# SwiGLU feed-forward on one core: the first 256 tokens of x loaded plainly and transposed on TensorE instead of by DMA

## The chip, the core and the metric

One core of one Trainium2 chip runs the kernel in a single launch. The metric is device time in microseconds (us). The kernel before takes 121.7 us, the median of three runs (121.63 to 121.72). Engines are named as the profile names them: PE is TensorE's matmuls, PEld its weight loads, DVE is VectorE, ACT is ScalarE, POOL is GpSimd, and SP is SyncE, which here only issues DMAs.

## The reference

```python
B, S, D, F = 1, 2048, 512, 1376        # everything in bfloat16
def reference(x, w_gate, w_up, w_down):
    g = silu(x @ w_gate)
    u = x @ w_up
    return (g * u) @ w_down
```

## The kernel before, in words

**Layout.** TensorE sums over the partition axis, so the kernel keeps x transposed in SBUF: xT_sb holds 4 blocks of 128 features (dk = 0 to 3) by 2048 tokens. The gate and up weights lie beside each other in w_sb, 4 blocks of 128 features each. The hidden activations hT_sb have hidden features on partitions, so they serve as the stationary side of the second product directly.

**Order of the work.** Tokens are taken in 4 chunks of 512. For each chunk and each of 10 hidden tiles of 128 features there is a gate group and an up group: four matmuls each, one per dk, 128 x 512, in one PSUM bank (line 260, in gu_matmuls). ACT takes the silu of the gate bank (line 215), DVE multiplies it with the up bank into hT_sb (line 222). The last 96 hidden features go in extra groups (lines 287 and 298). Then come 16 output tiles of 128 tokens, 11 matmuls each over the hidden features (line 315), a copy to bf16 (line 226, the last in two parts) and a store by SP (line 198). Eight PSUM banks are used in turn. Groups are numbered in the order of PE, and every engine's order is fixed when the program is built; semaphores count finished groups (s_P), finished ACT reads (s_A) and finished DVE results (s_D).

**Loads.** All are issued at the start, from two queues. ACT issues the gate and up weights of hidden tile 0 (wg0, wu0; 128 KB each, line 79). SP issues, in this order: x of tokens 0 to 255 (x0a) and of 256 to 511 (x0b), each as one transposing DMA (line 74); the other weights in slabs of growing size; the other three chunks of x, again as transposing DMAs; and w_down. Each load has a semaphore, and PE waits for it once, in `need`, ahead of the first matmul that reads it.

**The start on TensorE.** While the loads are under way PE multiplies a constant of ones: N_WARM = 9 dummies of 128 x 512 (line 268) and N_WARM_SHORT = 3 of 128 x 128 (line 271), into bank 7, and nothing reads their results. Then the first gate and the first up group run in two halves of 256 tokens:

```python
for n0, n1 in ((0, HT), (HT, SC)):      # HT = 256, SC = 512
    for g in groups[0:2]:               # gate 0, up 0
        gu_matmuls(g, n0, n1)
```

so that gate 0 and up 0 on tokens 0 to 255 need x0a only. From the third group on each matmul has 512 columns and the groups follow each other without a gap.

Of the kernel before, what the change touches and what calls it, by code (L numbers as in the profile page):

```python
# [5 lines left out]
ALU = mybir.AluOpType  # L6
BF16 = mybir.dt.bfloat16
FP32 = mybir.dt.float32

N_WARM = 9  # L10
N_WARM_SHORT = 3


def bass_standalone__swiglu_ffn__prompt_kernel(nc, x, w_gate, w_up, w_down, out):
    _, S, D = x.shape
    F = w_gate.shape[1]
    P = 128
# [4 lines left out]
    SC = 512  # L22
# [2 lines left out]
    NST = S // P  # L25
    LASTA = 384
    HT = SC // 2
    NB = 8
    NSG = 4
    NOS = 3  # L30
# [2 lines left out]
    xf = x[0]  # L33
# [8 lines left out]
    with ExitStack() as es:  # L42
        sb = lambda name, shape, dt: es.enter_context(nc.sbuf_tensor(name, shape, dt))
        ps = lambda name, shape, dt: es.enter_context(nc.psum_tensor(name, shape, dt))
        sem = lambda name: es.enter_context(nc.semaphore(name))

        xT_sb = sb("xT_sb", [P, KD, S], BF16)
# [7 lines left out]
        o_sb = [sb(f"o_sb{i}", [P, D], BF16) for i in range(NOS)]  # L55
        banks = [ps(f"bank{i}", [P, 512], FP32) for i in range(NB)]

        s_P = sem("s_P")
        s_A = sem("s_A")
        s_D = sem("s_D")  # L60
# [3 lines left out]
        def load_sem(name):  # L64
            loads[name] = sem(f"s_{name}")
            return loads[name]

        ones_w = nc.const_aps.tensor(1.0, [P, P], BF16)
        ones_m = nc.const_aps.tensor(1.0, [P, SC], BF16)
# [3 lines left out]
        def load_x(eng, name, t0, t1):  # L73
            eng.dma_start_transpose(
                xT_sb[:, :, t0:t1], xf[t0:t1, :]
            ).then_inc(load_sem(name), 16)
# [15 lines left out]
            load_slab(act, *slabs[0])  # L92

        def loads_on_sync(sp):
            load_x(sp, "x0a", 0, HT)
            load_x(sp, "x0b", HT, SC)
            for a, b in slabs[1:]:
                load_slab(sp, a, b)
            load_w(sp, "wut", w_up, F - (F - 32), F - 32, F)
            for c in range(1, NSC):  # L100
                load_x(sp, f"x{c}", c * SC, (c + 1) * SC)
            sp.dma_start(
                wd_sb[:, 0:NFF, :], w_down[0:NFF * P, :].rearrange("(k p) d -> p k d", p=P)
            ).then_inc(load_sem("wd"), 16)
            sp.dma_start(wd_sb[0:F_LAST, NFF, :], w_down[NFF * P:F, :]).then_inc(load_sem("wdt"), 16)
# [3 lines left out]
        groups = []  # L109
# [3 lines left out]
        def add_group(kind, **what):  # L113
            g = dict(kind=kind, at=len(groups), bank=banks[len(groups) % NB], readers=[], **what)
            groups.append(g)
            return g

        def add_op(eng, g, **what):
            n_read[eng] += 1
            op = dict(g=g, at=n_read[eng], **what)  # L120
            (act_ops if eng == "A" else dve_ops).append(op)
            g["readers"].append((eng, op["at"]))
            return op

        sg_reader = []
        n_sg = 0
# [34 lines left out]
        def plan_y(pi):  # L161
            g = add_group("Y", pi=pi)
            for c in (2 * pi, 2 * pi + 1):
# [4 lines left out]
                )  # L168
                t_ready[c] = d["at"]

        for c in range(NSC):
            for ft in range(NFF):
                plan_pair(c, ft)
            plan_x(c)
# [4 lines left out]
        for t in range(NST):  # L179
            ob = t % NOS  # L180
            need = 16 * n_store[ob]
            halves = [(0, D)] if t < NST - 1 else [(0, LASTA), (LASTA, D)]
            for c0, c1 in halves:
                g = add_group("O", t=t, c0=c0, c1=c1)
# [9 lines left out]
        def on_sync(sp):  # L194
            loads_on_sync(sp)
            for t, c0, c1, ob, eng, n in stores:
                sp.wait_ge(s_A if eng == "A" else s_D, n)
                sp.dma_start(of[t * P:(t + 1) * P, c0:c1], o_sb[ob][:, c0:c1]).then_inc(s_out[ob], 16)
            for i in range(NOS):
                sp.wait_ge(s_out[i], 16 * n_store[i])  # L200

        def on_scalar(act):
            loads_on_scalar(act)
            act.activation(adummy[:, 0:4], zero_c, ACT.Silu)  # L204
            for op in act_ops:
                act.wait_ge(s_P, op["g"]["at"] + 1)
                if op["kind"] == "silu":
                    if op["free"]:
                        act.wait_ge(s_D, op["free"])
                    fn = ACT.Silu  # L210
                else:
                    if op["stored"][1]:
                        act.wait_ge(*op["stored"])
                    fn = ACT.Copy
                act.activation(op["out"], op["src"], fn).then_inc(s_A, 1)  # L215
# [13 lines left out]
        def on_tensor(pe):  # L229
            landed = set()  # L230

            def need(name):
                if name not in landed:
                    pe.wait_ge(loads[name], 16)
                    landed.add(name)

            read = {"A": 0, "D": 0}

            def after(eng, n):
                if n > read[eng]:  # L240
                    pe.wait_ge(s_A if eng == "A" else s_D, n)
                    read[eng] = n

            def free(g):
                if g["at"] >= NB:
                    for eng, n in groups[g["at"] - NB]["readers"]:
                        after(eng, n)

            def gu_matmuls(g, n0, n1):
                c, ft = g["c"], g["ft"]  # L250
                if c > 0:
                    need(f"x{c}")
                elif n0 < HT:
                    need("x0a")
                if c == 0 and n1 > HT:
                    need("x0b")
                need(("wg" if g["kind"] == "G" else "wu") + str(slab_of[ft]))
                col = (0 if g["kind"] == "G" else UPH) + ft * P
                for dk in range(KD):
                    ins = pe.matmul(  # L260
                        g["bank"][:, n0:n1], lhsT=w_sb[:, dk, col:col + P],
                        rhs=xT_sb[:, dk, c * SC + n0:c * SC + n1], start=(dk == 0), stop=(dk == KD - 1),
                    )
                if n1 == SC:
                    ins.then_inc(s_P, 1)

            for i in range(N_WARM):
                pe.matmul(banks[NB - 1][:, :], lhsT=ones_w, rhs=ones_m, start=True, stop=True)  # L268

            for i in range(N_WARM_SHORT):  # L270
                pe.matmul(banks[NB - 1][:, 0:P], lhsT=ones_w, rhs=ones_m[:, 0:P], start=True, stop=True)  # L271

            for n0, n1 in ((0, HT), (HT, SC)):
                for g in groups[0:2]:
                    gu_matmuls(g, n0, n1)

            for g in groups[2:]:
                free(g)
                kind = g["kind"]
                if kind in "GU":  # L280
                    gu_matmuls(g, 0, SC)
                elif kind == "X":
                    c = g["c"]
                    need(f"wg{slab_of[NFF]}")
                    need("wut")
                    for dk in range(KD):
                        ins = pe.matmul(  # L287
                            g["bank"][:, :], lhsT=w_sb[:, dk, XC0:XC0 + P],
                            rhs=xT_sb[:, dk, c * SC:(c + 1) * SC],
                            start=(dk == 0), stop=(dk == KD - 1),  # L290
                        )
                    ins.then_inc(s_P, 1)
                elif kind == "Y":
                    need(f"wu{slab_of[NFF]}")
                    for dk in range(KD):
                        for c in (2 * g["pi"], 2 * g["pi"] + 1):
                            y0, y1 = yblk(c)
                            ins = pe.matmul(  # L298
                                g["bank"][y0:y1, :], lhsT=w_sb[:, dk, YC0:YC0 + 64],
                                rhs=xT_sb[:, dk, c * SC:(c + 1) * SC],  # L300
                                start=(dk == 0), stop=(dk == KD - 1),
                                tile_position=(0, y0), skip_group_check=True,
                            )
                    ins.then_inc(s_P, 1)
                else:
                    t, c0, c1 = g["t"], g["c0"], g["c1"]
                    c = t // TPC
                    need("wd")
                    after("D", h_ready[c])
                    for fk in range(NFT):  # L310
                        K = P if fk < NFF else F_LAST
                        if fk == NFF:
                            need("wdt")
                            after("D", t_ready[c])
                        ins = pe.matmul(  # L315
                            g["bank"][:, 0:c1 - c0], lhsT=hT_sb[0:K, fk, t * P:(t + 1) * P],
                            rhs=wd_sb[0:K, fk, c0:c1], start=(fk == 0), stop=(fk == NFT - 1),
                        )
                    ins.then_inc(s_P, 1)

        on_sync(nc.sync)
        on_scalar(nc.scalar)
        on_tensor(nc.tensor)
        on_vector(nc.vector)
# [28 lines left out]
```

## Time and profile before

| what | value |
|---|---|
| median of three runs | 121.7 us (121.63 to 121.72) |
| the profiled execution's own time | 121.83 us |
| its span, first to last instruction | 120.5 us |
| PE busy in the span | 116.8 us (97%) |
| DVE, ACT, POOL busy | 43.7, 30.3 and 0.2 us |
| granted TensorE clock, mean | 1.000 |
| DMA | 8.51 MB, mean 71 GB/s |

The profile is one execution. Its own time is 1.33 us above its span, which is time ahead of the first instruction and behind the last. A row of a timeline gives the start, the time that the merged row covers, the engine, the line, the operation with what it writes and reads, how many instructions were merged, and in brackets the engine's idle time ahead of the row with what ended it. SPq and ACTq are the instruction queues that issue DMAs. A matmul's busy time includes the way through the array, so matmuls of one row overlap: what a matmul costs in a stream is the distance between starts, not the mean duration. In tables by stage, each engine has its busy time and, in brackets, the instructions that were under way in that stage.

### The profile page before, as it was taken

How to read it: one execution, taken by the hardware profiler on the slowest of the kernel's cores; microseconds unless marked ns; L12 is line 12 of the kernel's file. 1: busy time of each engine (PE TensorE's matmuls, PEld its weight loads, DVE VectorE, ACT ScalarE, POOL GpSimd, SP SyncE). 2: the span in 40 equal slices, each digit the busy share in tenths (PEclk: the TensorE clock that was granted, in tenths of full speed). 3: DMA queues.
4: the chain of work that ended last, by engine and by line, in shares of the span. 5: the costliest groups of instructions: out<-in, count | busy, mean ns of one | idle time of the engine just before them, and what ended most of it. 6: DMA issues, size and time to landing. Idle time of an engine off the chain costs nothing.

```text
span 120.5 us, 1390 instructions
## 1 busy us (share of the span) xinstructions
PE 116.8 (97%) x549; PEld 53.9 (45%) x559; DVE 43.7 (36%) x64; ACT 30.3 (25%) x51; POOL 0.2 (0%) x4
## 2 busy tenths in 40 slices
PE   7899999999999999999999999999999999999993
PEld 2364444444444444444444444444444444444452
DVE  0024334444334444334444344467233223322420
ACT  4032333262332363332363332330000000000001
POOL 0000000000000000000000000000000000000000
DMA  4999999940000000000000000000211121112112
GB/s 79 227 301 375 284 234 145 322 139 0 0 0 0 0 0 5 0 0 3 3 0 0 0 5 0 0 0 0 87 44 44 45 91 44 44 60 71 44 44 87
DMA packets 18022, 8.51 MB, mean 71 GB/s; under 512 B 11520, under 2 KB 18016, under 8 KB 18016
## 3 DMA queue, kind: packets, MB, share of 16 engines
q1 hardware_dynamic: 16960, 8.16, 26.5%
q10 hardware_dynamic: 1056, 0.26, 1.0%
q8 instruction: 4, 0.07, 0.2%
q14 instruction: 2, 0.02, 0.0%
HBM read 4.23 MB, written 2.10 MB: 52 GB/s over the span
## 4 chain that ended last, share of the span: by engine, by line
PE 93%; DMA 4%; issue 1%; DVE 0%
PE bank L260 57%; PE bank L315 32%; DMA xT_sb<-in_x_dram 4%; PE bank L287 3%; PE bank L298 2%; DVE o_sb L226 0%
## 5 line engine op out<-in xcount | busy, mean ns | idle before, releaser
L260 PE MATMUL bank<-xT_sb,w_sb 128*128 128x512 bf16 (+1 forms) x321 | 69.5, 375 | 0.8 <-DMA xT_sb<-in_x_dram 0.5
L260 PEld LDWEIGHTS bank<-xT_sb,w_sb 128*128 128x128 bf16 x328 | 32.1, 98 | 37.7 <-DMA xT_sb<-in_x_dram 0.8
L222 DVE TENSOR_TENSOR hT_sb<-sg_sb,bank 128x512 bf16<-128x512 f32 x40 | 27.5, 688 | 46.3 <-PE bank L260 37.6
L315 PE MATMUL bank<-wd_sb,hT_sb 128*128 128x512 bf16 (+4 forms) x184 | 38.1, 366 | 0.2
L215 ACT ACTIVATE sg_sb<-bank 128x512 f32<-128x512 f32 x40 | 23.8, 596 | 43.6 <-PE bank L260 43.6
L315 PEld LDWEIGHTS bank<-wd_sb,hT_sb 128*128 128x128 bf16 (+1 forms) x187 | 17.8, 98 | 20.7 <-DVE hT_sb L222 0.4
L226 DVE CAST o_sb<-bank 128x512 bf16<-128x512 f32 (+1 forms) x16 | 10.7, 666 | 25.4 <-PE bank L315 25.3
L215 ACT ACTIVATE o_sb<-bank 128x384 bf16<-128x384 f32 x1 | 0.5, 490 | 38.2 <-PE bank L315 38.2
L268 PE MATMUL bank<-const-bfloat16-1.0 128*128 128x512 bf16 x9 | 4.0, 626 | 0.8 <-PEq L338 0.8
L287 PE MATMUL bank<-xT_sb,w_sb 128*128 128x512 bf16 x16 | 4.1, 379 | 0.1
L222 DVE TENSOR_TENSOR hT_sb<-sgx_sb,bank 32x512 bf16<-32x512 f32 x4 | 2.8, 692 | 3.5 <-ACT sgx_sb L215 3.5
L215 ACT ACTIVATE sgx_sb<-bank 32x512 f32<-32x512 f32 x4 | 2.3, 587 | 4.5 <-PE bank L287 4.5
L222 DVE TENSOR_TENSOR hT_sb<-sgy_sb,bank 64x512 bf16<-64x512 f32 x4 | 2.7, 684 | 0.1
L287 PEld LDWEIGHTS bank<-xT_sb,w_sb 128*128 128x128 bf16 x16 | 1.6, 98 | 1.9
L215 ACT ACTIVATE sgy_sb<-bank 64x512 f32<-64x512 f32 x4 | 2.4, 589 | 0.1
L268 PEld LDWEIGHTS bank<-const-bfloat16-1.0 128*128 128x128 bf16 x9 | 1.2, 138 | 2.7 <-issue 2.7
L298 PE MATMUL bank<-xT_sb,w_sb 128*64 128x512 bf16 x16 | 1.9, 382 | 0.0
L204 ACT ACT_TABLE_LOAD x1 | 1.3, 1283 | 1.8 <-issue 1.8
L298 PEld LDWEIGHTS bank<-xT_sb,w_sb 128*64 128x64 bf16 x16 | 0.8, 109 | 1.0 <-DVE hT_sb L222 0.4
L271 PEld LDWEIGHTS bank<-const-bfloat16-1.0 128*128 128x128 bf16 x3 | 0.4, 147 | 0.6 <-issue 0.6
L271 PE MATMUL bank<-const-bfloat16-1.0 128*128 128x128 bf16 x3 | 0.5, 311 | 0.0
L204 ACT ACTIVATE act_dummy<-const-float32-0.0 128x4 f32<-128x4 f32 x1 | 0.2, 205 | 0.0
(4 smaller groups left out, 0.4 us busy)
## 6 DMA issues: line engine op xcount, KB each, us to landing
out_dram<-o_sb SPq DMA_DIRECT2D x15, 128.0 KB, 1.7
wd_sb<-in_w_down_dram SPq DMA_DIRECT2D x1, 1280.0 KB, 6.5
w_sb<-in_w_gate_dram SPq DMA_DIRECT2D x1, 480.0 KB, 5.8
w_sb<-in_w_up_dram SPq DMA_DIRECT2D x1, 448.0 KB, 6.2
w_sb<-in_w_gate_dram SPq DMA_DIRECT2D x1, 384.0 KB, 4.5
w_sb<-in_w_up_dram SPq DMA_DIRECT2D x1, 384.0 KB, 5.0
w_sb<-in_w_gate_dram SPq DMA_DIRECT2D x1, 256.0 KB, 3.7
w_sb<-in_w_up_dram SPq DMA_DIRECT2D x1, 256.0 KB, 3.9
```

Of the source, the lines that this page charges most:

```text
L204: act.activation(adummy[:, 0:4], zero_c, ACT.Silu)
L215: act.activation(op["out"], op["src"], fn).then_inc(s_A, 1)
L222: ins = dve.tensor_tensor(op["out"], op["a"], op["b"], ALU.mult)
L226: ins = dve.tensor_copy(op["out"], op["src"])
L260: ins = pe.matmul(g["bank"][:, n0:n1], lhsT=w_sb[:, dk, col:col + P], rhs=xT_sb[:, dk, c * SC + n0:c * SC + n1], start=(dk == 0), stop=(dk ...
L268: pe.matmul(banks[NB - 1][:, :], lhsT=ones_w, rhs=ones_m, start=True, stop=True)
L271: pe.matmul(banks[NB - 1][:, 0:P], lhsT=ones_w, rhs=ones_m[:, 0:P], start=True, stop=True)
L287: ins = pe.matmul(g["bank"][:, :], lhsT=w_sb[:, dk, XC0:XC0 + P], rhs=xT_sb[:, dk, c * SC:(c + 1) * SC], start=(dk == 0), stop=(dk == KD - 1),
L298: ins = pe.matmul(g["bank"][y0:y1, :], lhsT=w_sb[:, dk, YC0:YC0 + 64], rhs=xT_sb[:, dk, c * SC:(c + 1) * SC], start=(dk == 0), stop=(dk == ...
L315: ins = pe.matmul(g["bank"][:, 0:c1 - c0], lhsT=hT_sb[0:K, fk, t * P:(t + 1) * P], rhs=wd_sb[0:K, fk, c0:c1], start=(fk == 0), stop=(fk == ...
```

## The change

The first 256 tokens of x no longer come by a transposing DMA. SP loads them with two plain DMAs of 128 tokens (128 KB each) into a new tile xn_sb. PE transposes the eight 128 x 128 blocks against an identity matrix into four PSUM banks (two blocks to a bank, as bf16), and DVE and ACT copy two banks each into xT_sb. POOL makes the identity, `ident`, with an affine select over the constant of ones. PE waits for it (s_I) ahead of the first transpose. Of the dummies, 4 wide ones stand ahead of the transposes and 3 short ones behind them. Gate 0 and up 0 now run on 128, 128 and 256 tokens, and the pieces on 128 wait for the copies where they waited for x0a. The four transpose groups are groups 0 to 3 in the numbering, so every later group uses a PSUM bank four places further on. The core of the diff:

```diff
-N_WARM = 9
-N_WARM_SHORT = 3
+N_WARM = 4
+N_FILL = 3
...
+    NXN = HT // P
...
+        xn_sb = sb("xn_sb", [P, NXN, D], BF16)
+        ident = sb("ident", [P, P], BF16)
...
         def loads_on_sync(sp):
-            load_x(sp, "x0a", 0, HT)
+            for i in range(NXN):
+                sp.dma_start(xn_sb[:, i, :], xf[i * P:(i + 1) * P, :]).then_inc(load_sem(f"xn{i}"), 16)
             load_x(sp, "x0b", HT, SC)
...
+        def tview(bank):
+            return bank[:, 0:P].bitcast(BF16).rearrange("p (k t) -> p k t", k=2)
...
+        xt_ready = {}
+        for i in range(NXN):
+            for h, eng in enumerate("DA"):
+                g = add_group("T", i=i, h=h)
+                op = add_op(
+                    eng, g, kind="copy", out=xT_sb[:, 2 * h:2 * h + 2, i * P:(i + 1) * P],
+                    src=tview(g["bank"]), stored=(None, 0),
+                )
+                xt_ready[i, h] = (eng, op["at"])
+        NT = len(groups)
...
+        def on_gpsimd(pool):
+            pool.affine_select(
+                ident[:, :], ones_w, pattern=[[-1, P]], compare_op=ALU.is_equal, fill=0.0,
+                base=0, channel_multiplier=1,
+            ).then_inc(s_I, 1)
...
                 for dk in range(KD):
+                    if c == 0 and dk % 2 == 0:
+                        for i in range(n0 // P, min(n1 // P, NXN)):
+                            after(*xt_ready[i, dk // 2])
...
-            for i in range(N_WARM):
-                pe.matmul(banks[NB - 1][:, :], lhsT=ones_w, rhs=ones_m, start=True, stop=True)
-
-            for i in range(N_WARM_SHORT):
-                pe.matmul(banks[NB - 1][:, 0:P], lhsT=ones_w, rhs=ones_m[:, 0:P], start=True, stop=True)
-
-            for n0, n1 in ((0, HT), (HT, SC)):
-                for g in groups[0:2]:
-                    gu_matmuls(g, n0, n1)
+            def warm(n, width):
+                for i in range(n):
+                    pe.matmul(banks[NB - 1][:, 0:width], lhsT=ones_w, rhs=ones_m[:, 0:width], start=True, stop=True)
+
+            warm(N_WARM, SC)
+            pe.wait_ge(s_I, 1)
+            for g in groups[:NT]:
+                need(f"xn{g['i']}")
+                for j in range(2):
+                    dk = 2 * g["h"] + j
+                    ins = pe.transpose(tview(g["bank"])[:, j, :], xn_sb[:, g["i"], dk * P:(dk + 1) * P], ident[:, :])
+                ins.then_inc(s_P, 1)
+            warm(N_FILL, P)
+
+            first = groups[NT:NT + 2]
+            for i in range(NXN):
+                for g in first:
+                    gu_matmuls(g, i * P, (i + 1) * P)
+            for g in first:
+                gu_matmuls(g, HT, SC)
```

In the built program the queue of POOL gains two instructions: the affine select, and ahead of it an instruction that the program names PseudoReloadLibraryIndex, for library 0. Nothing in the source names the second one; the builder puts it there.

More of the change, by code (lines that the diff above doesn't have):

```diff
@@ L56, in bass_standalone__swiglu_ffn__prompt_kernel @@
         banks = [ps(f"bank{i}", [P, 512], FP32) for i in range(NB)]
+        xn_sb = sb("xn_sb", [P, NXN, D], BF16)
+        ident = sb("ident", [P, P], BF16)
+        s_I = sem("s_I")
         s_P = sem("s_P")
@@ L252, in gu_matmuls @@
                     need(f"x{c}")
-                elif n0 < HT:
-                    need("x0a")
                 if c == 0 and n1 > HT:
@@ L265, in gu_matmuls @@
                     ins.then_inc(s_P, 1)
-            for i in range(N_WARM):
-                pe.matmul(banks[NB - 1][:, :], lhsT=ones_w, rhs=ones_m, start=True, stop=True)
-            for i in range(N_WARM_SHORT):
-                pe.matmul(banks[NB - 1][:, 0:P], lhsT=ones_w, rhs=ones_m[:, 0:P], start=True, stop=True)
-            for n0, n1 in ((0, HT), (HT, SC)):
-                for g in groups[0:2]:
-                    gu_matmuls(g, n0, n1)
-            for g in groups[2:]:
+            def warm(n, width):
[16 more added lines that the diff above has]
+                gu_matmuls(g, HT, SC)
+            for g in groups[NT + 2:]:
                 free(g)
@@ L321, in bass_standalone__swiglu_ffn__prompt_kernel @@
         on_sync(nc.sync)
+        on_gpsimd(nc.gpsimd)
         on_scalar(nc.scalar)
```

## The prediction, made before the result was known

> **What bounds the kernel now.** I read the page's list of groups first, then the chain of work that ended last over the first 30 us, the timeline of the start, and a table by stage of line 260. PE is busy 97% of the span, so only its idle time and its slow time can be saved. The first group row shows how little idle there is (the last column); the chain shows where it lies.
>
> ```profile
> L260 PE MATMUL bank<-xT_sb,w_sb 128*128 128x512 bf16 (+1 forms) x321 | 69.5, 375 | 0.8 <-DMA xT_sb<-in_x_dram 0.5
> ```
> ```profile
> 0.73 4.81 DMA xT_sb<-in_x_dram
> 5.54 0.05 issue
> 5.59 6.72 PE bank L260 x37
> ```
>
> The chain is one line: the transposing load of x0a, issued at 0.73, lands at 5.54, and real work starts at 5.59. Behind that PE runs without a gap that matters. So the end moves one to one with the time at which gate 0 and up 0 are done and the stream of 512-column matmuls begins, 7.62 us in this execution. Ahead of it:
>
> ```profile
> 0.30 0.10 POOL L338 MEMSET const-bfloat16-1.0<- 128x1 bf16 x1
> 0.73 2.66 SPq L74 DMA_TRANSPOSE xT_sb<-in_x_dram  x2
> 0.77 4.00 PE L268 MATMUL bank<-const-bfloat16-1.0 128*128 128x512 bf16 x9 [0.77 <-PEq L338]
> 1.76 1.28 ACT L204 ACT_TABLE_LOAD   x1 [1.76 <-issue]
> 4.56 0.52 PE L271 MATMUL bank<-const-bfloat16-1.0 128*128 128x128 bf16 x3
> ```
> ```profile
> 5.59:6.20 0.61, 0.61 (x3) 0.43 (x4) 1.00 1.37 231
> 6.20:6.85 0.65, 0.65 (x7) 0.59 (x6) 1.00 1.21 290
> 6.85:7.62 0.77, 0.77 (x9) 0.69 (x7) 1.00 1.08 293
> ```
>
> The table by stage has PE in its third column. [...] Nine wide dummies start between 0.77 and 4.56: (4.56 - 0.77) / 9 = 0.42 us for 512 columns. The first three 256-column matmuls take 0.61 / 3 = 0.20 us each; the other 13 of the 16 take (7.62 - 6.20) / 13 = 0.11 us. So PE runs at half rate until about 6.2 us, 5.4 us after its first dummy, then at full rate. A matmul of 128 columns costs 0.107 us slow; the 11 last ones of the kernel, 128 columns wide, cover 0.78 us with the way through the array, near 0.055 us each.
>
> **The change, part by part.** *Removed:* the 4.8 us of x0a, and five wide dummies (5 x 0.42 = 2.1 us); the four left end at 0.77 + 4 x 0.427 = 2.48.
>
> *Plain loads.* Each xn load is 128 KB. The nearest rows of that size are the store of an output tile (1.7 us to landing) and wg0 (2.7, with wu0, issued 0.5 later, at 4.1). I take 2.5 for xn0 and 2.7 for xn1, issued at 0.73 and 1.2 (an issue takes 0.44): they land at 3.2 and 3.9, between 2.4 and 5.3.
>
> *SP's queue.* One transposing issue (1.33) gives way to two plain ones (about 0.5 each), so everything behind is issued some 0.3 us earlier. No load but x0a made PE wait, so this costs and gains nothing; cover gone, it would be a gain of 0.3 at most.
>
> *The identity, on which every transpose waits.* The queue of POOL gets the select and, ahead of it, the library reload. The trace has neither. Select: 128 elements on each partition, between the memset (0.10) and a DVE multiply of 512 (0.69); I take 0.3, nearer the small row. Reload: below, nothing, if the library is there already, since then no code moves. Above, it is code fetched from memory. The table load of ACT (1.28) is the nearest by kind. But a fetch that starts at 0.7 shares the DMA engines with the loads, whose landings in this stage are 2.7 to 6.7 us; the 96 KB of w_down took 6.0, the 32 KB of w_up 5.7. I take 6.0, because even the small loads pay it beside the bulk. Then ident is ready at 0.7 + 6.0 + 0.3 = 7.0 and PE goes on at 7.05.
>
> [...]
>
> Queued behind the wait on PE are all the transposes and, through them, everything: the copies of DVE and ACT, their first multiply and silu. PE idles from 2.48 to 7.05. All data has landed by then.
>
> *Transposes, copies, first pieces, at slow rate.* Eight transposes of 128 columns, 8 x 0.107 = 0.86, to 7.91; three fillers, 0.32, to 8.23. A copy of 256 elements costs DVE 0.42 (between 0.29 for 128 and 0.69 for 512) and ACT 0.38 (0.49 for 384, 0.60 for 512, drawn on down). The first transpose pair ends at 7.47 (start 7.16, 0.31 through the array); its copy ends at 7.94, ACT's first at 8.11: in time for gate 0 at 8.25. The second copies end at 8.37 and 8.54, before the second pieces at 9.10. So transposes and copies cost only their 0.86 + 0.32; DVE and ACT were idle until 7.4 anyway. Sixteen pieces of 128 take 1.71, to 9.96.
>
> *The clock.* Below: it stays full once it would have been, through the idle stretch; then all 128-column steps cost half, the copies bind, and the 512 stream starts near 9.7, which is +2.1. Above: slow for 5.4 us from 7.05, to 12.5, as at the first start; the eight 256-column matmuls take 1.71 to 11.67, and 0.83 us of 512-column work at half rate loses 0.42: as if the stream had started at 12.09, +4.5. I take +3.7, two thirds of the way to the row that the trace does show.
>
> [...]
>
> *Sum,* against the profiled execution: 121.83 + 3.7 = 125.5. That execution is 0.13 above the median of the runs, so I forecast **125.4 us**. Its own range: 123.7 (clock at +2.1) to 127.3 (load 6.7 and select 0.69, so ident 1.1 later, with clock at +4.5).
>
> **Rivals.** *A, the identity is early* (faster). The library is resident, ident is ready near 1.0, and the loads set the pace: transposes of token block 0 at 3.25 to 3.68, of block 1 at 3.95 to 4.38, fillers to 4.70. Gate 0 starts at 4.70 instead of 5.59. Slow until 6.2, 14 of the 16 pieces are done by then; two more to 6.4, the 256-column part (0.87) to 7.26: 0.36 early, 121.3 by the median. With wu0 no sooner than 5.3 it is about the same; with early loads up to 0.9 early, 120.8. For it: POOL is busy 0.2 us and free. Against: the program does issue the reload.
>
> *B, the identity is early but the clock is late* (slower). The four dummies and the stop at 2.48 do not count towards full rate; 5.4 us count from the fillers at 4.38, to 9.8. Pieces to 6.41, the 256-column part to 8.12, and 1.68 us of the stream at half rate loses 0.84: as if it started at 8.96, +1.3, or 123.0. For it: PE was busy nearly all the time before full rate came, and is not now. Against: the trace does not show what counts.
>
> The main case turns into A below a reload of about 3 us: then transposes start near 4.1, gate 0 near 5.3, and the early start just pays for the longer slow stretch.
>
> **How the numbers follow.** The long reload, 125.4: 0.58. A: 0.24, nearly all more than 0.2% (0.24 us, about what a measurement of this kernel can tell from no change) faster. B with reloads of middling length: 0.14. Within 0.2%: 0.04. Faster is 0.24, same 0.04, slower 0.72. The range runs from 121.2, since A alone is over 2 in 10, to 127.3, and leaves out the early end of A and a reload beyond every landing row.
>
> **What would show it.** Right: POOL idle, then the select, at 6 to 7 us; PE's largest idle time ahead of the first transpose, released by POOL; starts of 128-column work 0.107 apart. A: PE's wait ahead of the first transpose ends with the load of xn0, near 3.2 us. B: full rate only near 9 to 10 us, with real work from 4.7. Wrong altogether: a wait on wu0, x0b or a copy in place of these, or a code fetch that delays the loads themselves.

## The result, and the profile after

The changed kernel takes 121.88 us (median of 19 runs, 121.13 to 123.19), the kernel before 121.47 us (19 runs, 121.10 to 121.72). The ratio is 1.0042, 95% interval 1.0023 to 1.0060: slower by 0.4%, where 3% was forecast. The more telling difference is the scatter: before spreads over 0.6 us (0.7 to 1.0 in the later series of runs), the change over 2.1 us, or 1.5 without its two longest runs. The ratio leaves these two out, 123.02 and 123.19 us, and the profiled execution is the first of them, with a span of 121.8, so its size is not that of the median. What it shows of the order of events is seen again below, in an execution of ordinary length (121.96 us).

First the engine on which the forecast rested, POOL, from the timeline of the changed kernel, and then PE up to the first pieces of gate 0 and up 0.

```profile
0.89 0.29 POOL L223 TENSOR_SCALAR_AFFINE_SELECT ident<-const-bfloat16-1.0 128x128 bf16<-128x128 bf16 x1 [0.38 <-POOLq L377]
```
```profile
0.84 1.87 PE L296 MATMUL bank<-const-bfloat16-1.0 128*128 128x512 bf16 x4 [0.84 <-PEq L377]
3.12 1.30 PE L304 MATMUL bank<-ident,xn_sb 128*128 128x128 bf16 x8 [0.41 <-DMA xn_sb<-in_x_dram]
4.21 0.52 PE L296 MATMUL bank<-const-bfloat16-1.0 128*128 128x128 bf16 x3
4.53 0.63 PE L287 MATMUL bank<-xT_sb,w_sb 128*128 128x128 bf16 x4
5.45 0.82 PE L287 MATMUL bank<-xT_sb,w_sb 128*128 128x128 bf16 x6 [0.29 <-DMA w_sb<-in_w_up_dram]
```

The select runs at 0.89, POOL having been idle for only 0.38 us after the memsets; the identity is there two microseconds before it is used. PE's wait ahead of the transposes ends with a load, x of block 0. Gate 0 starts at 4.53, a full microsecond before the 5.59 of the kernel before. But then up 0 waits for the up weights of tile 0. The page's row of these matmuls and the chain say the same: the wait on x has become a wait on the up weights, which land 0.13 us sooner than x0a did before (5.41 against 5.54).

```profile
L287 PE MATMUL bank<-xT_sb,w_sb 128*128 128x512 bf16 (+2 forms) x329 | 71.5, 378 | 0.7 <-DMA w_sb<-in_w_up_dram 0.3
```
```profile
1.30 4.11 DMA w_sb<-in_w_up_dram
5.41 0.05 issue
5.45 5.75 PE bank L287 x30
```

The wait explains why little is gained, not why time is lost. For that the table by stage has to be read as it was for the kernel before: PE's busy time and, in brackets, the matmuls under way.

```profile
5.45:6.71 1.26, 1.26 (x13) 1.00 1.27 276
6.71:8.41 1.70, 1.70 (x10) 1.00 1.10 338
8.41:9.27 0.86, 0.86 (x4) 1.00 1.09 366
9.53:10.61 1.08, 1.08 (x6) 1.00 1.09 374
```

Between 6.71 and 8.41 eight matmuls of 256 columns start, 0.21 us each; the other two of the ten began earlier. From 8.41 to 9.27 two of 512 start, 0.43 each; from 9.53 on five start in 1.08 us, 0.216 each. So PE goes to full rate at about 9.4 us in this execution, 3.2 us later than the 6.2 of the kernel before, and everything until then ran at half rate. The stream of 512-column matmuls begins at 8.41 where it began at 7.62, 0.79 us later, and the 1.0 us from there to 9.4 at half rate loses another 0.5. Together that is 1.3 us, the difference of the two spans (121.8 and 120.5). The page's busy time of the row has grown from 69.5 to 71.5 us for the same columns.

### The profile page after: what moved, and what is told of

The parts are those of the page before. It is cut to its first block, busy times and chain, and to the rows that moved or that the text cites. A ratio compares the mean times of both kernels' runs of the same rounds, so it can differ in the third digit from the quotient of the medians.

```text
span 121.8 us, 1422 instructions
## 1 busy us (share of the span) xinstructions
PE 117.7 (97%) x560; PEld 55.1 (45%) x570; DVE 44.3 (36%) x66; ACT 31.1 (26%) x53; POOL 0.5 (0%) x5
## 4 chain that ended last, share of the span: by engine, by line
PE 94%; DMA 3%; issue 1%; ACTq 0%; DVE 0%
PE bank L287 58%; PE bank L353 31%; DMA w_sb<-in_w_up_dram 3%; PE bank L325 3%; PE bank L336 2%; ACTq L84 0%; DVE o_sb L252 0%
## 5 line engine op out<-in xcount | busy, mean ns | idle before, releaser
L287 PE MATMUL bank<-xT_sb,w_sb 128*128 128x512 bf16 (+2 forms) x329 | 71.5, 378 | 0.7 <-DMA w_sb<-in_w_up_dram 0.3
L287 PEld LDWEIGHTS bank<-xT_sb,w_sb 128*128 128x128 bf16 x336 | 33.5, 102 | 37.9 <-DMA w_sb<-in_w_up_dram 0.6
L296 PE MATMUL bank<-const-bfloat16-1.0 128*128 128x512 bf16 (+1 forms) x7 | 2.4, 489 | 0.8 <-PEq L377 0.8
L325 PEld LDWEIGHTS bank<-xT_sb,w_sb 128*128 128x128 bf16 x16 | 1.6, 98 | 1.9
L252 DVE COPY xT_sb<-bank 128x256 bf16<-128x256 bf16 x2 | 0.6, 292 | 3.9 <-PE bank L304 3.9
L304 PE MATMUL bank<-ident,xn_sb 128*128 128x128 bf16 x8 | 1.2, 302 | 0.5 <-DMA xn_sb<-in_x_dram 0.4
L304 PEld LDWEIGHTS bank<-ident,xn_sb 128*128 128x128 bf16 x8 | 0.7, 127 | 1.7 <-issue 1.3
L296 PEld LDWEIGHTS bank<-const-bfloat16-1.0 128*128 128x128 bf16 x7 | 0.8, 136 | 1.4 <-issue 1.4
```

The lines of the kernel that those rows point to most:

```text
L252: ins = dve.tensor_copy(op["out"], op["src"])
L287: ins = pe.matmul(g["bank"][:, n0:n1], lhsT=w_sb[:, dk, col:col + P], rhs=xT_sb[:, dk, c * SC + n0:c * SC + n1], start=(dk == 0), stop=(dk ...
L296: pe.matmul(banks[NB - 1][:, 0:width], lhsT=ones_w, rhs=ones_m[:, 0:width], start=True, stop=True)
L304: ins = pe.transpose(tview(g["bank"])[:, j, :], xn_sb[:, g["i"], dk * P:(dk + 1) * P], ident[:, :])
L325: ins = pe.matmul(g["bank"][:, :], lhsT=w_sb[:, dk, XC0:XC0 + P], rhs=xT_sb[:, dk, c * SC:(c + 1) * SC], start=(dk == 0), stop=(dk == KD - 1),
```

## The experiments

Theory (clock): PE runs at half rate at first (0.43 us for 512 columns in the change, 0.216 from 9.4 us on), and idle time ahead of that puts the step to full rate off. The change leaves PE idle between its last wide dummy and the first transpose (0.41 us), between the transposes of the two blocks (0.11), and ahead of up 0 (0.29); full rate comes later, and at a time that differs from run to run. Rivals: the pieces, transposes and copies themselves cost the time; transposes do not count as busy; the wait on the up weights is all of it. And, of the forecast: the reload is cheap only because the code was there already.

**Dummies in three gaps.**

```diff
-N_WARM = 4
+N_WARM = 5
...
                 ins.then_inc(s_P, 1)
+                if g["i"] == 0 and g["h"] == 1:
+                    warm(2, P)
...
                 for g in first:
                     gu_matmuls(g, i * P, (i + 1) * P)
+                    if i == 0 and g is first[0]:
+                        warm(4, P)
```

> The changed kernel with dummies in the three gaps that its profile shows on PE: one more wide one ahead of the transposes, 2 short ones between the transposes of the two token blocks, 4 short ones between gate 0 and up 0 of block 0. Theory (clock): full rate comes later, and at a scattered time, because PE is no longer busy nearly all the time from 0.8 us on, and the changed kernel's times spread over 2 us for that reason. Then this one spreads over less than 1 us and its median falls to 121.0 to 121.3. Rival (pieces): the loss is in the 128-column pieces, the transposes and the copies themselves: then the median stays near 121.9. Rival (transposes do not count as busy): the spread shrinks only in part, median 121.5 to 121.8.

121.76 us (12 runs, 120.98 to 122.02), ratio to before 1.0002 (0.9984 to 1.0020). The spread halves, to 1.04 us, but the median misses the 121.0 to 121.3 of the theory. Its profiled execution, 120.98 us, goes to full rate at 4.8 us. Inconclusive by itself: either the clock is a part of it only, or one of the three fillers costs time, or transposes do not count as busy, since 121.76 lies in that rival's range too.

**The kernel before with fewer dummies.**

```diff
-N_WARM = 9
+N_WARM = 4
```

> The kernel before with 4 wide dummies in place of 9, so that PE stands idle from about 2.8 to 5.6 us, and nothing else changed. Theory (clock): real work starts at 5.6 as before, but at half rate for longer: median 122.0 to 122.8, with a spread of 1.5 us or more. Rivals (pieces, or transposes): dummies alone matter little, median within 0.2 of before, 121.3 to 121.7.

123.33 us (6 runs, 122.59 to 123.61), ratio 1.0124 (1.0100 to 1.0149): more than the theory asked for, though the spread, 1.0 us, is less than its 1.5. No piece, transpose or copy is in this kernel, and real work starts when it did before:

```profile
0.77 1.86 PE L268 MATMUL bank<-const-bfloat16-1.0 128*128 128x512 bf16 x4 [0.77 <-PEq L338]
2.42 0.53 PE L271 MATMUL bank<-const-bfloat16-1.0 128*128 128x128 bf16 x3
5.47 6.72 PE L260 MATMUL bank<-xT_sb,w_sb 128*128 128x256 bf16 x29 [2.52 <-DMA xT_sb<-in_x_dram]
```

PE is idle for 2.52 us, starts real work at 5.47, and does 29 matmuls in the 6.72 us from there, where the kernel before did 37 in as long. By the distances between starts full rate comes at about 9.6. Dummies that compute nothing are worth 1.2% here.

**The order gate, gate, up, up.**

```diff
-            for i in range(NXN):
-                for g in first:
+            for g in first:
+                for i in range(NXN):
                     gu_matmuls(g, i * P, (i + 1) * P)
```

> The changed kernel with the pieces on 128 tokens in another order: both of gate 0, then both of up 0, so that the second piece of gate 0 runs while the up weights of tile 0 are still under way. Theory (a wait on those weights, 0.3 us in the changed profile, has taken the place of the wait on x): the wait goes, the second piece of gate 0 (4 x 0.107 = 0.43 us) lies in it, median 121.4 to 121.6, still with a spread of about 2 us, since the clock is not helped. Rival (the clock is all of it): less than 0.15 from the changed kernel, 121.75 to 121.9, because the time at which full rate comes sets the end.

121.67 us (12 runs, 121.42 to 122.82), ratio 1.0022 (0.9995 to 1.0049), spread 1.4 us. In its profiled execution PE no longer waits for the up weights: from 4.93 on the chain is PE alone. The median lies between what the two theories asked for, and the interval takes in the changed kernel's ratio; not settled by this run.

**Order and dummies together**, with the first two gaps filled, run twice:

```diff
-N_WARM = 4
+N_WARM = 5
...
                 ins.then_inc(s_P, 1)
+                if g["i"] == 0 and g["h"] == 1:
+                    warm(2, P)
...
-            for i in range(NXN):
-                for g in first:
+            for g in first:
+                for i in range(NXN):
```

> The order of gate, gate, up, up together with the dummies in the first two gaps (one more wide one, 2 short ones). Theory (clock and the wait on the up weights both): 120.8 to 121.1, below both kernels, with a spread under 1 us. If only the clock matters: as with the dummies alone, 121.0 to 121.3. If neither: 121.7 to 121.9.

120.98 us (6 runs, 120.81 to 121.32), ratio 0.9944 (0.9927 to 0.9960): below both kernels.

> The kernel with the order gate, gate, up, up and the dummies in the first two gaps, once more, to see whether its times hold: 120.8 to 121.3 if the first median of 120.98 was no accident of the clock's phase; up to 122 in some runs if it was.

121.18 us (12 runs, 120.80 to 121.79), ratio 0.9980 (0.9962 to 0.9997). The gain holds, its first size did not: the two intervals do not meet, so two series of runs of one kernel differ by more than either interval says. In this second profiled execution full rate comes as early as 3.8 us, and then the loads bind:

```profile
PEld bank L287 <- DMA w_sb<-in_w_up_dram: 0.5, 1, 0.5
PEld bank L287 <- DMA xT_sb<-in_x_dram: 0.4, 1, 0.4
```

These rows of its list of waits (engine, for what, us in total, times, longest) are the up weights of tile 0 and x of tokens 256 to 511. The execution took 121.21 us, about as long as others with full rate at 6 (121.25 and 121.28, in the table below). An earlier clock was worth nothing here, since the data was late.

**Another library on POOL.**

```diff
+        pbc = sb("pbc", [P, 8], FP32)
...
         def on_gpsimd(pool):
+            pool.partition_broadcast(pbc[:, 0:4], zero_c[0:1, :], channels=P)
             pool.affine_select(
```

> The changed kernel with a small broadcast across partitions on POOL ahead of the affine select, into a tile that nothing reads. In the program, the one reload instruction then names another library, not the one that the changed kernel names. Theory (the reload of the changed kernel cost 0.38 us because the code was already there; a load of other code costs several us): the select runs at 6 us or later, PE waits for the identity, and the time is 124 to 128 us. Rival (a reload instruction is cheap whatever it names): the select runs before 2 us and the time stays at 121.5 to 122.3.

122.26 us (10 runs, 121.56 to 123.00), ratio 1.0054 (1.0031 to 1.0076), an interval that overlaps that of the changed kernel. The program's reload now names library 1, and POOL's timeline shows:

```profile
0.99 0.27 POOL L224 PARTITION_BROADCAST pbc<-const-float32-0.0  x1 [0.50 <-POOLq L379]
1.13 0.37 POOL L225 TENSOR_SCALAR_AFFINE_SELECT ident<-const-bfloat16-1.0 128x128 bf16<-128x128 bf16 x1
```

The theory falls: POOL is idle for 0.50 us instead of 0.38, whichever library is named. No load of code of any length shows.

The same execution settles a rival of the clock, the wait on the up weights. It is the change's own order of pieces with its four wide dummies, in an execution of 121.96 us, close to the changed kernel's median:

```profile
3.38 1.29 PE L306 MATMUL bank<-ident,xn_sb 128*128 128x128 bf16 x8 [0.69 <-DMA xn_sb<-in_x_dram]
4.78 4.50 PE L289 MATMUL bank<-xT_sb,w_sb 128*128 128x128 bf16 x30
```
```profile
6.48:7.33 0.85, 0.85 (x6) 1.00 1.08 309
7.82:8.68 0.86, 0.86 (x7) 1.00 1.00 317
```

From gate 0 on PE waits for nothing. Still four matmuls of 256 columns start between 6.48 and 7.33, 0.21 us each, and from 7.82 on four of 512 start in 0.86 us, 0.215 each: the distances in between put full rate at about 7.4. So it is late without any wait on the up weights.

**Transposes as dummies**, in the kernel before (N_WARM is 4 here, the short dummies follow, and POOL makes the identity as in the change):

```diff
+            pe.wait_ge(s_I, 1)
+            tb = banks[NB - 1][:, 0:P].bitcast(BF16).rearrange("p (k t) -> p k t", k=2)
+            for i in range(20):
+                pe.transpose(tb[:, i % 2, :], ident[:, :], ident[:, :])
```

> The kernel before with its last five wide dummies replaced by 20 transposes of 128 x 128 of a constant identity (20 x 0.107 = 2.1 us, the same stretch of PE time), with the 3 short dummies behind them. Loads and real work are those of before. Theory (transposes keep the clock as matmuls do): 121.3 to 121.8, as before. Rival (transposes do not count as busy): as with four wide dummies alone, 122.6 to 123.6.

121.59 us (12 runs, 121.14 to 121.90), ratio 1.0004 (0.9988 to 1.0019). In the profiled execution the transposes stand in the gap that four wide dummies alone leave, and full rate comes at about 6.5:

```profile
2.50 2.34 PE L281 MATMUL bank<-ident 128*128 128x128 bf16 x20
5.53 3.69 PE L268 MATMUL bank<-xT_sb,w_sb 128*128 128x256 bf16 x22 [0.37 <-DMA xT_sb<-in_x_dram]
```

The control has `pe.matmul(banks[NB - 1][:, 0:P], lhsT=ident[:, :], rhs=ident[:, :], start=True, stop=True)` in place of the transpose:

> The control of the run with transposes: the same 20 instructions as plain matmuls of 128 columns on the same constant. All theories: 121.3 to 121.8, as before; if this one is slow as well, it is the 128-column form or the wait on POOL and not the transpose.

121.55 us (12 runs, 121.26 to 122.15), ratio 1.0006 (0.9990 to 1.0021). Against the 1.0124 without these 20 instructions, transposes keep the clock as matmuls do, to within the 0.2% of these intervals. The rival falls.

**Which gap?** Three runs take the successful pair apart. The first has the fillers of the first two gaps in the change's own order of pieces:

```diff
                     gu_matmuls(g, i * P, (i + 1) * P)
-                    if i == 0 and g is first[0]:
-                        warm(4, P)
```

(against the kernel with three gaps filled).

> The changed kernel, its own order of pieces, with dummies in the first two gaps only (one more wide one, 2 short ones); the 4 short ones between gate 0 and up 0 of the run with three gaps filled are left out. Theory (those 4 were work in the way, 4 x 0.107 = 0.43 us at half rate, in runs where the up weights had landed): 121.2 to 121.5, below the 121.76 with three gaps filled. Rival (the order gate, gate, up, up is needed for the clock as well, because the wait on the up weights is what delays full rate): 121.7 to 121.9, as with three gaps filled or above it.

121.07 us (12 runs, 120.72 to 121.79), ratio 0.9963 (0.9942 to 0.9984). So the order is not needed. That the four short dummies ahead of up 0 stood in the way of real work is seen in the profiled execution with three gaps filled, where the up weights had landed at 4.6:

```profile
5.04 0.40 PE L296 MATMUL bank<-const-bfloat16-1.0 128*128 128x128 bf16 x4
```

There they put up 0 off by 0.24 us, from 5.04 to 5.28, at full rate; at half rate they would take 0.43. The medians differ by 0.69 and the two intervals meet at 0.9984, so the size is not settled.

> The order gate, gate, up, up with one more wide dummy ahead of the transposes, without the 2 short ones between the transposes. Theory (idle time on PE delays full rate, and the first gap is the longest, 0.4 to 0.6 us): most of the way from the order alone (121.67) to both gaps filled (121.1): 121.1 to 121.4. Rival (the second gap, 0.26 us, counts as much): 121.5 to 121.7.

With N_WARM = 5 and the order gate, gate, up, up, without the 2 short dummies: 121.17 us (12 runs, 120.68 to 121.78), ratio 0.9971 (0.9953 to 0.9990). Filling the first gap is enough.

> Order gate, gate, up, up, both gaps filled, and a sixth wide dummy, which ends at about 3.4 us, where x of block 0 has landed. Theory (nearly no idle time is left ahead of the real work): 120.9 to 121.2, spread no more than 0.8 us. Rival (the sixth dummy holds up the transposes by up to 0.2 us and the clock gains nothing): 121.2 to 121.4.

With N_WARM = 6, the order, and the 2 short ones: 121.12 us (12 runs, 120.55 to 121.66), ratio 0.9969 (0.9951 to 0.9987). No better and no worse; the spread, 1.1 us, misses the 0.8.

**One dummy.** The last run takes the changed kernel and one number:

```diff
-N_WARM = 4
+N_WARM = 5
```

> The changed kernel with N_WARM = 5 in place of 4, one more wide dummy ahead of the transposes (0.43 us at half rate, ending at about 3.0, before x of block 0 lands), and nothing else changed. Theory (the idle time ahead of the first transpose is what delays full rate): most of the way from 121.9 to 121.1, so 121.1 to 121.4. Rival (the second gap, ahead of the transposes of block 1, has to be filled too): 121.5 to 121.8.

121.18 us (12 runs, 120.48 to 121.67), ratio 0.9965 (0.9944 to 0.9986): from 0.4% slower than before to 0.35% faster by one matmul whose result nothing reads. PE in its profiled execution (120.95 us) and the stages that stand against those of the changed kernel above:

```profile
0.84 2.29 PE L296 MATMUL bank<-const-bfloat16-1.0 128*128 128x512 bf16 x5 [0.84 <-PEq L377]
3.21 0.58 PE L304 MATMUL bank<-ident,xn_sb 128*128 128x128 bf16 x4
3.95 0.61 PE L304 MATMUL bank<-ident,xn_sb 128*128 128x128 bf16 x4 [0.16 <-DMA xn_sb<-in_x_dram]
```
```profile
5.45:6.71 1.26, 1.26 (x19) 1.00 1.01 234
6.71:8.41 1.70, 1.70 (x11) 1.00 1.06 312
```

The transposes do not start sooner, 3.21 against 3.12. But between 5.45 and 6.71 nineteen matmuls are under way where the change has thirteen: full rate is there at about 5.45 instead of 9.4.

All kernels in one table. The time of full rate is read off the distances between the starts of PE's matmuls, and belongs to the one profiled execution; each ratio is to runs of the kernel before in the same series.

| kernel | wide dummies | full rate from, us | that execution, us | median, us | ratio to before |
|---|---|---|---|---|---|
| before | 9 | 6.2 | 121.83 | 121.47 | 1 |
| before, 20 transposes | 4 | 6.5 | 121.90 | 121.59 | 1.0004 |
| before, 20 short matmuls | 4 | 5.4 | 121.80 | 121.55 | 1.0006 |
| before, 4 dummies | 4 | 9.6 | 123.47 | 123.33 | 1.0124 |
| change | 4 | 9.4 | 123.02 | 121.88 | 1.0042 |
| change, order | 4 | 7.8 | 122.10 | 121.67 | 1.0022 |
| change, other library | 4 | 7.4 | 121.96 | 122.26 | 1.0054 |
| change, order and first gap | 5 | 6.2 | 121.25 | 121.17 | 0.9971 |
| change, order, both gaps, six wide | 6 | 6.0 | 121.28 | 121.12 | 0.9969 |
| change, one more dummy | 5 | 5.45 | 120.95 | 121.18 | 0.9965 |
| change, two gaps | 5 | 5.45 | 121.02 | 121.07 | 0.9963 |
| change, three gaps | 5 | 4.8 | 120.98 | 121.76 | 1.0002 |
| change, order and two gaps | 5 | 4.5 | 121.00 | 120.98 | 0.9944 |
| the same, run again | 5 | 3.8 | 121.21 | 121.18 | 0.9980 |

In the seven rows of the change from 9.4 down to 5.45 the time of the execution follows the full-rate time at (123.02 - 120.95) / (9.4 - 5.45) = 0.52 us for each us (0.49 without the longest): the half that half rate costs. The rows between lie within 0.1 us of that line. What follows the start is the same: in ten of the fourteen executions the span lasts 112.9 us from the start of the 512-column stream (120.5 - 7.62 before, 119.7 - 6.81 with one more dummy).

In the last three the clock comes sooner still and the time falls no further. Two of them wait for loads: the last as shown above, the other 0.25 us for the up weights of tile 1 at 7.71. The one with three gaps filled waits for no weights; its transposes start 0.2 us later than with one more dummy (3.40 against 3.21), and its four dummies take 0.24 us. The kernel before with 20 short matmuls gains nothing from full rate at 5.4 either: it then waits for up weights until 8.50 and loses 0.5 us. By the same 0.52 the scatter of the changed kernel, 1.5 us without its two longest runs, would stand for some 3 us of scatter in when the clock comes; that is an estimate from the line.

## Why the prediction was wrong

**The step that failed** is the price of the reload: "I take 6.0, because even the small loads pay it beside the bulk." It was taken to be a fetch of code through the busy DMA engines, by the landing rows. That was the author's assumption, and no run shows such a fetch: the two queues of kind instruction moved the same 6 packets and 0.09 MB before, with the change and with the other library. POOL was idle for 0.38 us ahead of the select, and for 0.50 with another library, so the reload cost no more than that. The bound below, nothing, was the right end. The main case, with 0.58 of the chance, its wait on the identity and its 125.4 us go with it. That the kernel did come out slower is luck: what slows it is not that wait. (The lower end of the range, 121.83 + 2.1 - 0.13, is 123.8 and not 123.7, which changes nothing.) Whether code had been moved before the kernel started, no run here can tell.

**What came in its place** is rival B in its mechanism and rival A in its times. The loads landed a little early, 2.2 and 2.5 us after issue where 2.5 and 2.7 were taken; transposes of block 0 started at 3.12 (3.25 in the sum), of block 1 at 3.81 (3.95), gate 0 at 4.53 (4.70). The row costs were right: 0.107 us for a transpose, 0.38 for a copy on ACT; DVE's copy from bf16 took 0.29 where 0.42 was taken. SP's later loads were issued 0.3 to 0.4 us earlier and changed nothing.

The rest of A, 16 pieces without a stop, failed on the up weights, 4.1 us to landing. A had allowed for them at 5.3 and called it about the same; they landed at 5.41. B put full rate at 9.8 us and the time at 123.0; the profiled execution has 9.4 and 123.02. That the two agree so closely is luck, for B was one price, and the runs are a scatter: the best of the changed kernel's runs, 121.13, is that of A, the worst, 123.19, that of B, and the median 121.88 lies between. The prediction had the right two ends, gave them 0.38 together, and lost them to a load that no run shows.

B's reason stands in part. It said that the dummies before the stop do not count and that the count starts at the fillers. The run with one more dummy shows that a stop shorter by 0.3 us is enough to bring full rate back to where it was or sooner, which it could not do if nothing ahead of the stop counted: its transposes begin only 2.2 us ahead of full rate. Nor is the 5.4 us, which the main case and both rivals took over from the row of the kernel before, a constant. From the first dummy to full rate it was 3.0 to 5.7 us in the ten executions above in which PE stood idle for 0.51 us or less in all in between, and 6.6 to 8.8 in the four with 0.71 us or more (the kernel before with 4 dummies, the change, the order alone, the other library). From the fillers, B's 5.4 us was 5.2 in the profiled execution of the change, but 3.0 with the other library.

The time from the first dummy to full rate varies among those ten as well: 3.0 us in the second run of order and two gaps, 5.2 us with six wide dummies, where PE had no stop at all.

**What stays open:** by what rule PE's recent busy time sets the moment of full rate. That idle time on PE is the cause was shown by taking away dummies in the kernel before (1.0124) and adding one in the changed one (1.0042 to 0.9965). Filling the gap ahead of the first transpose alone is enough; whether filling the others alone would do as well was not run. The total of idle time separates the fast cases from the slow ones (0.51 us or less against 0.71 or more), but these are fourteen executions, and no run tried the values between. Why 0.43 us of dummy moves full rate by two to four microseconds (5.45 against 7.4 and 9.4) was not measured. Nor does any run show a phase of the clock, which the expectation of the second run of order and two gaps supposes.

## What to carry to other kernels

Dummies that keep TensorE busy while the first data is under way are part of the kernel's speed (without five of nine, the kernel before was 1.2% slower): when a change moves the first real work, recount them up to the last microsecond before it, and leave no stop in between, but put none where real work could stand. Read the rate of the array off the distance between starts, since the granted clock read 1.00 in every stage while 512 columns took 0.43 us and then 0.216, and take many runs: a scatter that widens from 0.6 to 1.5 us or more is itself a finding. And before giving an unseen operation the price of its worst row, ask what else in the profile would have had to show it.

## What was not expected of the hardware

- The reload instruction on POOL cost at most 0.38 us with library 0 and 0.50 us with library 1; the select of 128 x 128 took 0.29 and 0.37 us.
- One dummy matmul of 0.43 us moved the median by 0.7 us (121.88 with four, 121.18 with five, in two series of runs whose medians of the kernel before were 121.47 and 121.45).
- The load of tile 0's up weights, 128 KB, issued 0.5 us behind that of its gate weights on the same queue, took 4.1 us to landing where the gate weights took 2.6; in the execution with the other library the two took 3.2 and 2.9. Which transfer came late at the start differed between the two: there the transposes started at 3.38 and gate 0 at 4.78, and PE did not wait for these weights.
